# First batch of a fused attention and expert kernel: two exponentials ahead of the router's square, the second batch's maxima behind the choice of the expert, and the rounding of W2 on GpSimd behind the router's index

## The chip, the cores and the metric

One Trainium2 chip, one of its cores, one program. The metric is the device time of a run in microseconds (us). The kernel before takes 421.18 us (median of 3 runs, 421.13 to 421.21).

The engines are named as in the profile: PE is TensorE's matmul stream and PEld its weight loads, DVE is VectorE, ACT is ScalarE, POOL is GpSimd, SP is SyncE, which here only issues transfers. Each engine works its own queue in order; the order is the one in which the program text issues the instructions.

## The reference, cut to what matters

```python
# for each of 8 batches and 8 heads, seq 576, head_dim 64, 32 memory slots
a = exp(phi - phi.max(over seq)); a = a / (a.sum(over seq) + 1e-9)
k_m = a.T @ k ; v_m = a.T @ v                    # 32 x 64 each
s = softmax(q @ k_m.T / 8)                       # 576 x 32
attn_out = s @ v_m                               # 576 x 64
# then tokens x = attn_out laid out as (8*576, 512), 8 experts, F = 1024
logits = (x/|x|) @ (emb/|emb|).T / tau
e = argmax(logits); gate = softmax(logits)[e]
out[mask_e] = gate * (relu(x[mask_e] @ w1[e]) @ w2[e])
```

## The kernel before

The kernel goes through the eight batches one after the other. For batch b it computes with one expert, the one that the batch's tokens name (`choose`, line 160: the tokens are counted on PE, the largest count is read into a register, and W1 and W2 of that expert are loaded). What would be left over for other experts is done in a branch at the end (`rest`), which these inputs don't enter.

The heavy part is two chains of matmuls per batch: `first` (line 617) computes relu(x W1) in 16 steps, and `second` (line 639) multiplies it with W2, token tile by token tile: first the half tile (line 670, W2 unrounded, 32 matmuls), then four whole tiles of 24 matmuls each (line 681). For those, W2 is held as two rounded parts, `wh` (rounded) and `wl` (the rest), in eight chunks; chunk f is needed by the matmuls of step f:

```python
def split_w(self, copy=None):                 # L595
    j = self.halves
    x, h, l = self.w2s[:, j], self.wh[:, j], self.wl[:, j]
    (copy or self.nc.scalar.copy)(h, x)                                        # L598
    self.nc.gpsimd.tensor_tensor(out=l, in0=x, in1=h.bitcast(F32), op=ALU.subtract)  # L599
```

`steps` (line 690) writes the order by hand: two lists, `first` (16 places) and `second` (40 places), hold what is issued behind each step of the two matmul chains, so that softmax, the router and the next batch's attention run beside the matmuls. In batches 1 to 7 all eight `split_w` round on GpSimd (first[0] to first[7]). In batch 0 they round on ScalarE, in first[9], [11], [13], [15] and second[0] to [3], and GpSimd only subtracts.

The start (`moe_linformer`, line 902 on) has no matmul chain to hide behind. Its order: the weights phi of batch 0 are loaded, `largest` (line 411) takes the maxima on VectorE, `softmax` (line 417) the exponentials on ScalarE, for two groups of heads; behind each group one step of `router` (line 313): the square of the expert embeddings on ScalarE (line 319), then the normalisation of them on VectorE (lines 38 to 44 and 324 to 326). `turn` (line 444) transposes the exponentials on PE and copies them back on ScalarE (`eT`); `slots` (line 454) forms k_m and v_m from them and from the keys and values (`kx`, `kl`) in `acc0t` and `acc0m`; then come `block`, `flip`, the scores, the softmax of the first 128 tokens, `attend(0)`, and `choose((0,))`, which releases the load of W1. Batch 1's exponentials, transposes and slots follow, then batch 0's remaining tokens. `warm` (line 344) issues matmuls whose result nobody reads.

`late` (line 225) is the tail of the router for the gates: `root` and `gates` (line 200), handed out over first[3] to first[8] in batch 0. Its last part takes the index of each token's expert, `idx` (line 218), on VectorE from `m` (line 217).

Of the kernel before, what the change touches and what calls it, by code (L numbers as in the profile page):

```python
# [13 lines left out]
ALU = mybir.AluOpType  # L14
# [7 lines left out]
N, DM, E, FF = B * S, H * D, 8, 1024  # L22
NG = 2
# [23 lines left out]
class Tokens:  # L47
# [152 lines left out]
    def gates(self):  # L200
        k, nc, b = self.k, self.nc, self.b
        m, n, lg = self.m, self.n, self.lg
        wk = k.wk.tile

        def b3(x):
            return x.unsqueeze(2).broadcast_to((P, NT, E))

        self.l = l = wk([P, NT, E], F32, tag="l", name=f"l{b}")
        nc.vector.tensor_tensor(out=m, in0=m, in1=n, op=ALU.mult)
        nc.vector.tensor_tensor(out=l, in0=lg, in1=b3(n), op=ALU.mult)  # L210
        nc.vector.tensor_tensor(out=l, in0=l, in1=b3(m), op=ALU.subtract)
        yield
        nc.scalar.activation(l, l, AF.Exp)

        eq = wk([P, NT, E], F32, tag="eq", name=f"eq{b}")
        nc.vector.tensor_tensor(out=eq, in0=self.oh, in1=k.rev8.unsqueeze(1).broadcast_to((P, NT, E)), op=ALU.mult)
        nc.vector.tensor_reduce(out=m, in_=eq, axis=AX.X, op=ALU.max)
        nc.vector.tensor_scalar(out=k.idx[:, b], in0=m, scalar1=-1.0, scalar2=float(E), op0=ALU.mult, op1=ALU.add)
        z = wk([P, NT], F32, tag="zz", name=f"zz{b}")
        nc.vector.tensor_reduce(out=z, in_=l, axis=AX.X, op=ALU.add)  # L220
        nc.vector.tensor_scalar(out=z, in0=z, scalar1=1e-9, scalar2=None, op0=ALU.add)
        nc.vector.reciprocal(out=k.gate[:, b], in_=z)
        yield
# [7 lines left out]
class Kernel:  # L231
# [458 lines left out]
    def steps(self, b, t, u):  # L690


        first, second = ([[] for _ in range(n)] for n in (16, 40))

        for j in range(8):
            copy = self.nc.gpsimd.tensor_copy if b else None
            at = first[j if b else 9 + j * 2] if b or j < 4 else second[j - 4]
            at.append(lambda copy=copy: self.split_w(copy))
        if not b:
            late = t.late()  # L700
            first[2].append(lambda: t.attend(3, 4))
            first[3].append(lambda: t.norm(3, 4))
            first[4] += [t.total, lambda: self.load_kv(2)]

            for f in range(3, 9):
                first[f].append(lambda: next(late))
            first[12] += [lambda: self.keep(0), lambda: self.load_q(2)]
        if u:
            c, o = b + 1, 0 if b else 3
            if not b:  # L710
                first[9].append(lambda: self.scores(c))
            for k in range(2):
                first[(3 + k if b else 9 + 2 * k)].append(lambda k=k: self.results(c, k))

            places = (first[6], first[8], first[10], first[12]), (first[12], first[14], second[0], second[3])
            if not b:
                places = (second[3], second[3], second[3], second[7]), (second[7], second[7], second[7], second[10])
            all = slice(0, BL)
            for g in range(NG):
                work = u.weigh((g,), all)  # L720
                places[g][0].append(lambda g=g: u.fill((g,), all, [self.sT[:, i] for i in range(NG)]))
                for at in places[g][1:]:
                    at.append(lambda work=work: next(work, None))
            for at, g in zip((second[0], second[3]) if b else (second[7], second[10]), range(NG)):
                at.append(lambda g=g: (u.divide((g,), all), u.lay(g), u.turn((g,), all)))
            o = 0 if b else 7
            second[17 + o].append(lambda: u.attend(0, 1, pt=self.mm))
            second[19 + o].append(lambda: u.attend(2, 3))
            second[21 + o].append(lambda: u.attend(4))
            second[22 + o] += [lambda: self.load_w2(u.choose()), self.parts, lambda: self.keep(c)]  # L730
            second[23 + o] += [u.owner, u.flags]
            for n, i in enumerate(((0, 1), (2, 3), (4,)) if b else ((2, 3), (4,), (0, 1))):
                second[24 + n + o].append(lambda i=i: u.norm(*i))
            after = u.late()
            for n in (27, 28, 29, 30, 31, 32):
                second[n + o].append(lambda: next(after))
            second[32 + o].append(lambda: list(after))
            m = b + 2
            if m < B:
                for g in range(NG):  # L740
                    second[11 + 3 * g + o].append(lambda g=g: self.softmax(m, (g,)))
                second[18 + o].append(lambda: self.shares(m))
                second[(28 if b else 25) + o].append(lambda: [self.turn(m, i, min(i + 4, 9)) for i in (0, 4, 8)])
                at = second[(31 if b else 28) + o]
                at += [lambda: self.slots(m), lambda: self.blocks(m, 0), lambda: self.blocks(m, 1, True)]
                for g in range(NG):
                    second[(35 + 2 * g if b else 31 + g) + o].append(lambda g=g: self.flip(m, g))
        return first, second
# [153 lines left out]
def moe_linformer(ctx, tc, phiT, qT, kv, kvt, emb, tau, w1, w2, out):  # L902
    k = Kernel(ctx, tc, phiT, qT, kv, kvt, emb, tau, w1, w2, out)
# [13 lines left out]
    router = k.router()  # L917
    for g in range(NG):
        k.largest(0, g)
        k.softmax(0, (g,))  # L920
        next(router)
    for i in (0, 4, 8):
        k.turn(0, i, min(i + 4, 9))
        if i < 8:
            k.warm(2)
    k.shares(0)
    k.load_phi(1)
    t = Tokens(k, 0, k.pt)
    keys, values = slice(0, 1), slice(1, 2)
    for ks in ((0, 1), (4,), (2,), (3,)):  # L930
        k.slots(0, accs, ks=ks, first=0 in ks, last=3 in ks)
        if ks[0] < 3:
            k.warm(1)
    k.block(0, 0)
    k.load_kv(1)
    k.flip(0, 0, keys)
# [2 lines left out]
    first, others = slice(0, 4), slice(4, BL)  # L939
# [12 lines left out]
    k.warm(5, 2)  # L952
    t.divide(range(NG), first)
    t.turn(range(NG), first)
    k.largest(1, 0)
    k.softmax(1, (0,))
    t.attend(0, pt=lambda shape, name: k.mm(shape, name, 2), turned=False)
    e = t.choose((0,))
    k.largest(1, 1)
    k.softmax(1, (1,))  # L960
    k.load_q(1, (0,))
    t.turned(0)
    for i in (0, 4, 8):
        k.turn(1, i, min(i + 4, 9))
        k.turns += not i
        if not i:
            k.warm(8, hot=t.spare)
    t.fill(range(NG), others, ts)
    weights = [t.weigh((g,), others) for g in range(NG)]
    for g in range(NG):  # L970
# [22 lines left out]
    for b in range(B):  # L993
        u = Tokens(k, b + 1, k.pt) if b < B - 1 else None
        left = k.batch(b, t, u)
        t = u
# [30 lines left out]
```

## Time and profile before

| | |
|---|---|
| median of 3 runs | 421.18 us (421.13 to 421.21) |
| the profiled execution's own time | 421.38 us |
| its span, first to last instruction | 419.0 us |
| PE busy | 405.8 us (97%) |
| DVE / ACT / POOL busy | 262.4 / 173.2 / 168.6 us |
| mean granted TensorE clock | 0.992 |
| first matmul of `first`, batch 0 | 34.48 us |
| first whole tile of `second`, batch 0 | 54.12 us |

The times of the table's last rows count from the start of the span. The profiled execution took 2.4 us more than its span, and 0.20 us more than the median of the runs.

### The profile page before, as it was taken

How to read it: one execution, taken by the hardware profiler on the slowest of the kernel's cores; microseconds unless marked ns; L12 is line 12 of the kernel's file. 1: busy time of each engine (PE TensorE's matmuls, PEld its weight loads, DVE VectorE, ACT ScalarE, POOL GpSimd, SP SyncE). 2: the span in 40 equal slices, each digit the busy share in tenths (PEclk: the TensorE clock that was granted, in tenths of full speed). 3: DMA queues.
4: the chain of work that ended last, by engine and by line, in shares of the span. 5: the costliest groups of instructions: out<-in, count | busy, mean ns of one | idle time of the engine just before them, and what ended most of it. 6: DMA issues, size and time to landing. Idle time of an engine off the chain costs nothing. (4 is left out here: it accounts for less than half of the span.)

```text
span 419.0 us, 9431 instructions
## 1 busy us (share of the span) xinstructions
PE 405.8 (97%) x3489; PEld 329.5 (79%) x3489; DVE 262.4 (63%) x839; ACT 173.2 (41%) x476; POOL 168.6 (40%) x196
## 2 busy tenths in 40 slices
PE   6989999999999999999999999999999999999993
PEld 2458878788877978879787988879788888879783
DVE  4597796679664795648772695648955495745000
ACT  4466742375225722356313642357223661145110
POOL 0032380387132942259130960339331681359000
PEclk9899999999999999999999999999999999999998
DMA  8979926896769824995469926798349404690101
GB/s 272 345 281 344 362 85 156 283 371 268 154 214 398 334 50 118 344 372 218 75 206 378 364 89 148 241 386 318 60 127 366 155 0 96 201 398 10 37 36 47
DMA packets 69858, 91.19 MB, mean 218 GB/s; under 512 B 41800, under 2 KB 47688, under 8 KB 69808
## 3 DMA queue, kind: packets, MB, share of 16 engines
q1 hardware_dynamic: 66928, 82.00, 59.3%
q0 software_dynamic: 2688, 8.26, 5.3%
q8 instruction: 29, 0.48, 0.5%
q10 hardware_dynamic: 192, 0.28, 0.3%
q14 instruction: 21, 0.17, 0.1%
HBM read 71.19 MB, written 19.33 MB: 216 GB/s over the span
## 5 line engine op out<-in xcount | busy, mean ns | idle before, releaser
L628 PE MATMUL ph<-aT,gh 128*128 128x288 f32 x512 | 103.2, 297 | 0.5 <-DVE gl L612 0.5
L681 PE MATMUL py<-wh,hh 128*128 128x512 f32 x248 | 102.3, 413 | 0.0
L681 PE MATMUL py<-wl,hh 128*128 128x512 f32 x248 | 97.0, 391 | 0.3 <-POOL wl L599 0.3
L681 PE MATMUL py<-wh,hl 128*128 128x512 f32 x248 | 97.1, 392 | 0.0
L599 POOL TENSOR_TENSOR wl<-w2s,wh 128x512 fp32r<-128x512 f32 x64 | 83.4, 1306 | 16.8 <-ACT wh L598 12.3
L628 PEld LDWEIGHTS ph<-aT,gh 128*128 128x128 f32 x512 | 81.7, 188 | 3.0 <-DVE gl L612 1.4
L628 PE MATMUL ph<-aT,gl 128*128 128x288 f32 x256 | 75.4, 294 | 0.0
L634 DVE SCALAR_TENSOR_TENSOR hl<-ph,hh 128x288 fp32r<-128x288 f32 x128 | 56.0, 449 | 22.6 <-ACT hh L631 16.6
L631 ACT ACTIVATE hh<-ph 128x288 fp32r<-128x288 f32 x128 | 52.4, 417 | 32.9 <-PE ph L628 32.3
L686 ACT ACTIVATE ys<-py,gate 128x512 f32<-128x512 f32 (+1 forms) x39 | 25.0, 641 | 96.0 <-issue 48.3
L789 POOL DMA_DIRECT2D out_dram<-ys x28 | 15.5, 553 | 118.2 <-ACT ys L686 110.5
L681 PEld LDWEIGHTS py<-wh,hh 128*128 128x128 f32 x248 | 46.6, 188 | 12.0 <-issue 3.9
L681 PEld LDWEIGHTS py<-wh,hl 128*128 128x128 f32 x248 | 46.5, 188 | 10.2
L681 PEld LDWEIGHTS py<-wl,hh 128*128 128x128 f32 x248 | 46.7, 188 | 8.5 <-POOL wl L599 0.7
L628 PEld LDWEIGHTS ph<-aT,gl 128*128 128x128 f32 x256 | 48.0, 188 | 0.0
L589 POOL TENSOR_TENSOR aT<-aw,aT 128x576 fp32r<-128x576 f32 (+3 forms) x20 | 24.5, 1240 | 43.9 <-PE py L681 33.8
L612 DVE TENSOR_TENSOR gl<-pg,gh 128x512 fp32r<-128x512 f32 x32 | 20.0, 683 | 34.9 <-ACT gh L611 34.9
L598 POOL CAST wh<-w2s 128x512 fp32r<-128x512 f32 x56 | 37.5, 669 | 0.6 <-DMA w2s<-w 0.6
L670 PE MATMUL py<-w2s,h 128*64 128x256 f32 x256 | 29.4, 382 | 0.0
L427 ACT ACTIVATE ex<-ex,nm 128x576 f32<-128x576 f32 x16 | 12.3, 770 | 30.9 <-DVE nm L412 29.9
L670 PEld LDWEIGHTS py<-w2s,h 128*64 128x64 f32 x256 | 17.7, 137 | 9.4 <-DVE hl L634 1.1
L119 DVE TENSOR_REDUCE lg<-po 128x8 f32<-128x16 f32 x40 | 6.8, 173 | 28.1 <-PE po L114 28.0
(168 smaller groups left out, 522.6 us busy)
## 6 DMA issues: line engine op xcount, KB each, us to landing
kx<-kv SPq DMA_DIRECT2D x32, 512.0 KB, 7.0
w2s<-w SPq DMA_DIRECT2D x32, 512.0 KB, 10.2
w1s<-w SPq DMA_DIRECT2D x28, 512.0 KB, 6.5
out_dram<-ys POOLq DMA_DIRECT2D x28, 256.0 KB, 6.0
qt<-qT SPq DMA_DIRECT2D x12, 576.0 KB, 8.4
ad<-aw SPq DMA_DIRECT2D x8, 576.0 KB, 13.0
td<-x SPq DMA_DIRECT2D x56, 72.0 KB, 2.2
ea<-td SPq DMA_DIRECT2D x7, 512.0 KB, 4.1
```

What stands on the lines that cost most here:

```text
L427: nc.scalar.activation(x, x, AF.Exp, bias=nm[:, g : g + 1], accum_out=sm[:, g : g + 1])
L589: self.nc.gpsimd.tensor_tensor(out=al, in0=a, in1=ah.bitcast(F32), op=ALU.subtract)
L598: (copy or self.nc.scalar.copy)(h, x)
L599: self.nc.gpsimd.tensor_tensor(out=l, in0=x, in1=h.bitcast(F32), op=ALU.subtract)
L612: nc.vector.tensor_tensor(out=self.gl[:, g, f], in0=ps[g], in1=self.gh[:, g, f].bitcast(F32), op=ALU.subtract)
L628: nc.tensor.matmul(p, lhsT=w[:, g, fs], rhs=x[:, g, to], start=g == 0 and k == 0, stop=g == 1 and k == 2)
L631: nc.scalar.activation(self.hh[:, f, to], p, AF.Relu)
L634: nc.vector.scalar_tensor_tensor(out=self.hl[:, f, to], in0=p, scalar=0.0, in1=self.hh[:, f, to].bitcast(F32), op0=ALU.max, op1=ALU.subtract)
L670: nc.tensor.matmul(p[64 * j : 64 * j + 64], lhsT=self.h4[:, f], rhs=self.w2s[:, f, d * j : d * j + d], start=f == 0, stop=f == 7,)
L681: nc.tensor.matmul(p, lhsT=h[:, f, to], rhs=w[:, f], start=f == 0 and k == 0, stop=f == 7 and k == 2)
L686: nc.scalar.activation(y[:, :d], p, AF.Copy, scale=gate[:, i : i + 1])
L789: eng.dma_start(self.out[r : r + P], y)
```

## The change

In the start: both exponentials of batch 0 are issued ahead of the router's square, which moves behind the first transposes; the normalisation moves behind `shares(0)`; some `warm` counts change. For batch 1, both maxima and both exponentials move behind `choose((0,))` and `turned(0)`, and the eight warm matmuls are divided into four and three. In batch 0 the rounding of W2 moves from ScalarE to GpSimd, in first[9] to first[15] and second[0], and `idx` of batch 0 moves from VectorE to GpSimd, which in GpSimd's queue puts it ahead of all eight `split_w`.

```diff
-        nc.vector.tensor_scalar(out=k.idx[:, b], in0=m, scalar1=-1.0, ...)
+        (nc.vector if b else nc.gpsimd).tensor_scalar(out=k.idx[:, b], in0=m, scalar1=-1.0, ...)
...
         for j in range(8):
-            copy = self.nc.gpsimd.tensor_copy if b else None
-            at = first[j if b else 9 + j * 2] if b or j < 4 else second[j - 4]
-            at.append(lambda copy=copy: self.split_w(copy))
+            at = first[j] if b else first[9 + j] if j < 7 else second[0]
+            at.append(lambda: self.split_w(self.nc.gpsimd.tensor_copy))
...
     for g in range(NG):
         k.largest(0, g)
         k.softmax(0, (g,))
-        next(router)
     for i in (0, 4, 8):
         k.turn(0, i, min(i + 4, 9))
+        if not i:
+            next(router)
         if i < 8:
-            k.warm(2)
+            k.warm(2 if i else 4)
     k.shares(0)
+    next(router)
...
         if ks[0] < 3:
-            k.warm(1)
+            k.warm(2 if ks[0] == 2 else 1)
...
     t.turn(range(NG), first)
-    k.largest(1, 0)
-    k.softmax(1, (0,))
     t.attend(0, pt=lambda shape, name: k.mm(shape, name, 2), turned=False)
     e = t.choose((0,))
-    k.largest(1, 1)
-    k.softmax(1, (1,))
+    t.turned(0)
+    for g in range(NG):
+        k.largest(1, g)
+        k.softmax(1, (g,))
     k.load_q(1, (0,))
-    t.turned(0)
+    k.warm(4, hot=t.spare)
     for i in (0, 4, 8):
         k.turn(1, i, min(i + 4, 9))
         k.turns += not i
         if not i:
-            k.warm(8, hot=t.spare)
+            k.warm(3, hot=t.spare)
```

## Rows read from the trace of the kernel before

**Rows 1.** Busy time by stretch of the span (us from its start): length, busy us of PE, PEld, DVE, ACT and POOL with their instruction counts, then granted clock (1.00 is full), DMA share, GB/s. The middle of the kernel.

```profile
55.00:60.00 5.00, 4.71 (x21) 3.61 (x20) 4.84 (x7) 1.37 (x2) 5.00 (x4) 1.00 0.00 0
62.00:110.00 48.00, 48.00 (x427) 39.85 (x426) 36.46 (x111) 20.92 (x59) 20.90 (x24) 1.00 0.81 252
302.00:350.00 48.00, 48.00 (x426) 39.84 (x425) 31.91 (x103) 20.60 (x57) 21.49 (x24) 1.00 0.47 152
```

**Rows 2.** Instructions in order of time, start of the kernel: start us, us, engine, line, operation, out<-in, count, and in brackets the engine's idle time before it and what ended it.

```profile
6.00 0.75 DVE L412 TENSOR_REDUCE nm<-ex 128x1 f32<-128x576 f32 x1 [1.06 <-DMA ex<-phiT]
7.73 0.63 ACT L319 ACTIVATE w2s<-sT 8x512 f32<-8x512 f32 x1 [1.90 <-DMA sT<-emb]
8.36 0.76 ACT L427 ACTIVATE ex<-ex,nm 128x576 f32<-128x576 f32 x1
8.48 0.14 DVE L38 TENSOR_SCALAR eng<-es 8x1 int32<-8x1 int32 x1 [1.74 <-ACT w2s L319]
9.26 1.12 PE L449 MATMUL te<-ident,ex 128*128 128x128 f32 x4 [2.23 <-ACT ex L427]
10.90 0.47 DVE L326 TENSOR_SCALAR w2s<-sT,en 8x512 f32<-8x512 f32 x1
14.54 0.43 PE L469 MATMUL acc0t<-kx,eT 128*32 128x128 f32 x8
```

**Rows 3.** The same columns as rows 1, half-microsecond stretches of the start.

```profile
10.00:10.50 0.50, 0.50 (x3) 0.27 (x2) 0.40 (x4) 0.08 (x1) 0.00 (x0) 0.50 1.04 420
12.50:13.00 0.50, 0.50 (x17) 0.30 (x9) 0.00 (x0) 0.00 (x0) 0.00 (x0) 0.93 1.04 373
21.50:22.00 0.50, 0.00 (x0) 0.00 (x0) 0.42 (x3) 0.50 (x1) 0.00 (x0) 1.00 1.04 426
```

**Rows 4.** The issue of the fourth transfer of batch 0's keys and values on SP's queue, from the order of time, and the same transfer in the list of transfers, whose last number is us from issue to landing; then the same two for the two halves of batch 0's W1.

```profile
5.28 0.61 SPq L375 DMA_DIRECT2D kx<-kv  x1
kx<-kv SPq DMA_DIRECT2D x1, 512.0 KB, 6.7
23.71 1.37 SPq L397 DMA_DIRECT2D w1s<-w  x2
w1s<-w SPq DMA_DIRECT2D x2, 1024.0 KB, 5.4
```

**Rows 5.** In order of time, from the choice of the expert to batch 0's first heavy matmul.

```profile
20.74 0.71 DVE L412 TENSOR_REDUCE nm<-ex 128x1 f32<-128x576 f32 x1
22.53 0.14 DVE L166 TENSOR_SCALAR seli<-ki 1x1 int32<-1x1 int32 x1
22.60 0.73 DVE L412 TENSOR_REDUCE nm<-ex 128x1 f32<-128x576 f32 x1
23.41 0.78 ACT L427 ACTIVATE ex<-ex,nm 128x576 f32<-128x576 f32 x1 [1.05 <-issue]
25.54 1.08 PE L469 MATMUL acc0t<-kx,eT 128*32 128x128 f32 x32
30.00 1.09 PE L609 MATMUL pg<-w1s,vT 64*32 64x512 f32 x16
34.48 0.53 PE L628 MATMUL ph<-aT,gh 128*128 128x288 f32 x2
```

**Rows 6.** In order of time, the end of the router in batch 0, and GpSimd around it.

```profile
34.56 1.58 POOL L589 TENSOR_TENSOR aT<-aw,aT 128x288 fp32r<-128x288 f32 x2 [2.28 <-ACT aT L588]
39.78 0.46 DVE L634 SCALAR_TENSOR_TENSOR hl<-ph,hh 128x288 fp32r<-128x288 f32 x1 [0.80 <-ACT hh L631]
45.88 0.20 DVE L217 TENSOR_REDUCE m<-eq 128x5 f32<-128x40 f32 x1
46.64 1.28 POOL L599 TENSOR_TENSOR wl<-w2s,wh 128x512 fp32r<-128x512 f32 x1 [10.50 <-ACT wh L598]
50.97 8.68 POOL L599 TENSOR_TENSOR wl<-w2s,wh 128x512 fp32r<-128x512 f32 x6 [0.66 <-ACT wh L598]
```

**Rows 7.** In order of time on GpSimd, batch 1's rounding and subtracting, the first chunk, the fifth chunk's rounding, and a later rounding beside the VectorE instruction of its time; and, from the groups of lines, a small `tensor_scalar` on GpSimd (count, busy us, mean ns).

```profile
85.62 0.61 POOL L598 CAST wh<-w2s 128x512 fp32r<-128x512 f32 x1 [0.61 <-DMA w2s<-w]
86.32 1.28 POOL L599 TENSOR_TENSOR wl<-w2s,wh 128x512 fp32r<-128x512 f32 x1
93.34 0.61 POOL L598 CAST wh<-w2s 128x512 fp32r<-128x512 f32 x1
96.70 1.16 DVE L72 TENSOR_TENSOR x<-x,mx 128x576 f32<-128x576 f32 x1
97.18 1.16 POOL L598 CAST wh<-w2s 128x512 fp32r<-128x512 f32 x1
L438 POOL TENSOR_SCALAR rs<-sm 128x1 f32<-128x1 f32 x1 | 0.2, 221 | 0.1
```

**Rows 8.** In order of time, VectorE, GpSimd and PE while the first whole tile of `second` runs in batch 0.

```profile
53.74 1.72 DVE L72 TENSOR_TENSOR x<-x,mx 128x576 f32<-128x576 f32 x1
54.12 0.50 PE L681 MATMUL py<-wh,hh 128*128 128x512 f32 x1
57.83 1.81 POOL L599 TENSOR_TENSOR wl<-w2s,wh 128x512 fp32r<-128x512 f32 x1
59.70 0.50 PE L681 MATMUL py<-wl,hh 128*128 128x512 f32 x1 [0.29 <-POOL wl L599]
60.01 0.76 DVE L84 TENSOR_TENSOR x<-x,z 128x576 f32<-128x576 f32 x1
```

More of the change, by code (lines that the diff above doesn't have):

```diff
@@ L217, in gates @@
         nc.vector.tensor_reduce(out=m, in_=eq, axis=AX.X, op=ALU.max)
-        nc.vector.tensor_scalar(out=k.idx[:, b], in0=m, scalar1=-1.0, scalar2=float(E), op0=ALU.mult, op1=ALU.add)
+        (nc.vector if b else nc.gpsimd).tensor_scalar(out=k.idx[:, b], in0=m, scalar1=-1.0, scalar2=float(E), op0=ALU.mult, op1=ALU.add)
         z = wk([P, NT], F32, tag="zz", name=f"zz{b}")
```

## The prediction, made before the changed kernel was run

> **What bounds the kernel now.** I read the stretches first. PE is busy without a gap in the stretches after 62 us, of which an early and a late one stand here [rows 1]. Whatever moves PE's stream at 62 us therefore moves the end by as much, and nothing after it can give it back or absorb it. So only two places count: the start, until the first heavy matmul at 34.48 [rows 5], and the gap that the stretch 55 to 60 shows [rows 1].
>
> The order of time shows the start as one chain. ScalarE waits until 7.73 for the embeddings, squares them, and only then takes the second exponential, at 8.36; its maximum had been ready at 6.75 (6.00 + 0.75). PE has nothing for 2.23 before the transposes at 9.26 [rows 2]. After that pause the granted clock is 0.50 (1.2 GHz), and only from 12.5 on is it near 1.00 (2.4 GHz) again [rows 3]. The slots of batch 0 end with the group at 14.54 [rows 2], the expert is chosen at 22.67 (22.53 + 0.14), and the heavy matmuls follow 12 us later [rows 5].
>
> The gap at 59.70 is PE waiting for the last `wl` chunk: GpSimd subtracts six chunks in a row from 50.97 to 59.65 [rows 6, 8]. So GpSimd is already the limit there, by a little. This is the fact that decides the forecast.
>
> **The start, step by step.** With both exponentials first, the second starts at 6.8 instead of 8.36, and its transposes, 0.90 behind it (9.26 - 8.36) [rows 2], at 7.7 instead of 9.26. PE's pause of 2.23 loses 1.55 to the earlier exponential and most of the rest to the two added warm matmuls, so I expect the clock to stay at 2.4 GHz. The square now falls between two copies of `eT` on ScalarE: 0.63, hidden by the transposes that the second copy waits for. The normalisation takes VectorE 2.9 (8.48 to 10.90 + 0.47) [rows 2]; behind a square that ends near 8.8 it ends near 11.8, and VectorE's next work is the product of the slots, which end after 12. If that cover failed, it would cost what sticks out, some tenths.
>
> How far does that carry? The last slots group needs the fourth `kx` transfer, issued at 5.28 and landed 6.7 later, at 12.0 [rows 4]. PE could be there at about 12, does two warm matmuls, and runs the group at 12.1 to 12.2 instead of 14.54: 2.35 earlier. Below, the transfer bounds it; above, nothing gained there is 0. I take 2.35, since each step has its row, and it carries to the choice of the expert: 20.3 instead of 22.67.
>
> Then the second move takes some back. Before, one maximum of batch 1 (0.71) ran ahead of `lg`, in time in which VectorE would otherwise have waited for PE, and only one stood behind the choice; the second exponential started at 23.41, which is 0.74 behind the choice [rows 5]. Now two maxima stand behind it (0.71 + 0.73), and the second exponential starts 0.78 behind the first: 20.3 + 0.74 + 0.78 = 21.85, which is 1.55 earlier than 23.41, not 2.35. Behind the exponential come the transposes, the slots of batch 1 (25.54) and the projection (30.00), all in one chain. VectorE's own chain, from the second maximum (22.60) on, is 0.71 later relative to the choice by the maximum that now stands in it, so it too comes 1.6 earlier. W1's first half landed at 29.1 (23.71 + 5.4) [rows 4], 0.9 before its use at 30.00; issued behind the choice, it moves by 2.35 if the transfers before it are done, and needs to move by only 0.6 to be there at 28.5. So the heavy matmuls start at **33.0 instead of 34.48: 1.5 gained**. Bounds: 0.5 (a copy or transfer late on the way) and 2.35 (the second move costs nothing).
>
> **The rounding, step by step.** GpSimd is idle from 36.1 (34.56 + 1.58) until 46.64 [rows 6]. In the new order its next instruction is `idx`, and all eight chunks stand behind that. `idx` needs `m`, which VectorE has at 46.08 (45.88 + 0.20). VectorE's way there starts behind `hl` at 39.78, which itself waited for ScalarE and, through it, for PE [rows 6], so `m` moves with PE's stream: 44.58. Hand-over 0.07 (GpSimd to PE takes 0.06: 57.83 + 1.81 to 59.70 [rows 8]), `idx` 0.22 (by a like instruction [rows 7]): the first rounding starts at 44.87.
>
> A chunk costs GpSimd a rounding and a subtraction: in batch 1 the first and the fifth rounding start (93.34 - 85.62)/4 = 1.93 per chunk apart [rows 7]. The eighth subtraction ends 7 x 1.93 + 0.70 + 1.28 = 15.49 after the first rounding starts: 60.36.
>
> To this come collisions with VectorE. The instruction of line 72 has two SBUF operands; it took 1.72 beside GpSimd's subtractions, where the like line 84 took 0.76 with GpSimd free of them, and the subtraction that ran beside the second group's line 72 took 1.81 instead of 1.28, so 0.53 lost; in batch 1 a rounding lost 0.55 (1.16 - 0.61) in the same way [rows 7, 8]. In the new order both line 72s and the first line 84 (60.01, moved 1.5 earlier, to 58.5) lie within GpSimd's stretch: three collisions, 1.6. Two would be 1.1, four (the second group's line 84 too) 2.1.
>
> The Trainium skill, "SBUF — State Buffer", section "SBUF: two separate sides", says that VectorE instructions with two SBUF inputs and GpSimd's take turns at one port pair under a lock held for the whole instruction. By that rule each collision could cost GpSimd the whole 0.76 of the VectorE instruction, 2.3 for three; the rows show 0.53 to 0.55, and the rows decide.
>
> So the last chunk is ready at 60.36 + 1.6 = 61.98 and PE goes on at 62.04, where it did at 59.70 [rows 8]. Before that, PE is at the whole tile at 52.6 (54.12 - 1.5) and waits for the sixth, seventh and eighth chunks in turn. ScalarE is relieved of eight roundings, which buys nothing, since PE waits for no ScalarE work in this stretch.
>
> **The sum.** 62.04 - 59.70 = **2.3 us later**, the gain of 1.5 already counted. On the profiled execution that is 421.38 + 2.3 = 423.7; on the median, 0.20 lower, 423.5.
>
> **The rivals.**
>
> *The router doesn't hold the rounding back: faster.* If `m` came early, or GpSimd could round as W2 arrives, PE would find every chunk ready. Then 1.5 of the start and the 0.29 which PE waited for the last chunk before are gained: 421.2 - 1.8 = 419.4. The point from which it decides: to have the last chunk by 59.65, with three collisions, the first rounding must start by 59.65 - 15.49 - 1.6 = 42.6, which is 2.3 before my 44.87. For it: GpSimd idles for 10 us before its first subtraction [rows 6]. Against it: GpSimd works its queue in order, `idx` stands ahead of the rounding there, and nothing in the change brings `m` forward relative to PE's stream.
>
> *The second move costs nothing and two collisions happen:* gain of 2.35 instead of 1.5, 0.5 less lost: 2.3 - 0.85 - 0.5 = 0.95 later, 422.1, on the edge between same and slower.
>
> *The clock falls in PE's wait.* By the pace above PE waits 1.2 to 1.9 before each of the last three chunks: GpSimd takes 1.93 for a chunk, and with a collision 2.5, where PE uses one up in three matmuls, some 0.7 ((59.70 - 54.12)/8). After 2.23 idle microseconds the granted clock was at 0.50 from about 9.3 to 12.6 [rows 2, 3]. If it falls here for as long, 3.3 us at half speed cost up to 1.65 more: 425.1. Part of it would hide in the waits. Against it: between 21.5 and 22.0 PE did nothing, and the clock stayed at 1.00 [rows 3].
>
> *The start's gain is mostly lost* (a late transfer or a copy on ScalarE that PE waits for): 0.5 instead of 1.5, 424.5.
>
> **How the numbers follow.** The forecast 0.55, the clock 0.13, the lost start 0.10, the cheap second move 0.10, the unheld rounding 0.12. About 0.2% (0.84 us) is what a measurement can tell from no change. Faster is the unheld rounding: 0.12. Same takes half of the cheap second move, and the part of the forecast with no collision losses and a little more gain: 0.12. Slower is the rest, 0.76. The forecast's own range is 422.5 to 424.3 (one to four collisions, the start 0.3 either way). The range for 8 in 10 leaves out the unheld rounding and reaches to the others: 421.6 to 425.2.
>
> **What the new profile would show.** The second exponential at 6.8, transposes at 7.7, clock 1.00 from 9 to 13, the last slots group near 12.2; the choice near 20.3, batch 1's second exponential near 21.9, the first heavy matmul near 33.0. GpSimd idle until about 44.6, then `idx`, then sixteen instructions without a pause until 61 to 62; PE waiting for `wl` three times between 56 and 62. I am wrong if the rounding starts before 43, if PE's stream begins before 32, or if PE doesn't wait for `wl`.

## The result, and the profile after

The changed kernel takes 423.75 us (median of 8 runs, 422.03 to 425.39), the kernel before beside it 420.38 us (8 runs, 418.55 to 421.21): ratio 1.0084, interval 1.0055 to 1.0114. It is slower by 0.8%. Run again beside the experiments it gave 424.37 against 420.92, ratio 1.0095 (1.0065 to 1.0124). Its profiled execution took 424.92, with a span of 423.1 (before: 421.38 and 419.0).

The start after the change, in order of time (columns as in [rows 2]; the last three rows answer to the choice, to batch 1's second exponential and to the first heavy matmul in [rows 5]):

```profile
6.51 0.78 ACT L427 ACTIVATE ex<-ex,nm 128x576 f32<-128x576 f32 x1 [0.67 <-DVE nm L412]
7.43 0.66 PE L449 MATMUL te<-ident,ex 128*128 128x128 f32 x4
9.71 0.43 PE L469 MATMUL acc0t<-kx,eT 128*32 128x128 f32 x8 [0.73 <-DMA kx<-kv]
12.32 0.43 PE L469 MATMUL acc0t<-kx,eT 128*32 128x128 f32 x8
20.31 0.14 DVE L166 TENSOR_SCALAR seli<-ki 1x1 int32<-1x1 int32 x1
21.92 0.76 ACT L427 ACTIVATE ex<-ex,nm 128x576 f32<-128x576 f32 x1
32.89 0.53 PE L628 MATMUL ph<-aT,gh 128*128 128x288 f32 x2
```

The second exponential runs at 6.51 instead of 8.36, the last slots group at 12.32 instead of 14.54, the choice ends at 20.45 instead of 22.67, and the heavy matmuls start at 32.89 instead of 34.48: 1.59 gained.

GpSimd and VectorE around the rounding of W2, in order of time, and then PE; these answer to [rows 6] and [rows 8]:

```profile
44.58 0.20 POOL L218 TENSOR_SCALAR idx<-m 128x5 f32<-128x5 f32 x1 [10.03 <-DVE m L217]
44.85 0.61 POOL L598 CAST wh<-w2s 128x512 fp32r<-128x512 f32 x1
51.52 1.67 DVE L72 TENSOR_TENSOR x<-x,mx 128x576 f32<-128x576 f32 x1
52.53 1.14 POOL L598 CAST wh<-w2s 128x512 fp32r<-128x512 f32 x1
54.71 0.95 DVE L72 TENSOR_TENSOR x<-x,mx 128x576 f32<-128x576 f32 x1
55.00 1.14 POOL L598 CAST wh<-w2s 128x512 fp32r<-128x512 f32 x1
57.85 0.80 DVE L84 TENSOR_TENSOR x<-x,z 128x576 f32<-128x576 f32 x1
58.12 1.66 POOL L599 TENSOR_TENSOR wl<-w2s,wh 128x512 fp32r<-128x512 f32 x1
60.41 1.27 POOL L599 TENSOR_TENSOR wl<-w2s,wh 128x512 fp32r<-128x512 f32 x1
57.54 0.50 PE L681 MATMUL py<-wl,hh 128*128 128x512 f32 x1 [0.85 <-POOL wl L599]
59.83 0.79 PE L681 MATMUL py<-wl,hh 128*128 128x512 f32 x1 [1.25 <-POOL wl L599]
60.42 0.63 PE L681 MATMUL py<-wh,hl 128*128 128x512 f32 x1
61.74 0.79 PE L681 MATMUL py<-wl,hh 128*128 128x512 f32 x1 [0.26 <-POOL wl L599]
```

GpSimd waits 10.03 for `m`, rounds from 44.85 without a pause, and PE waits for the sixth, seventh and eighth chunk. The last one is read at 61.74, where it was 59.70 before: 2.04 later. The matmuls from 59.83 on take 0.79 and 0.63 instead of 0.50 and 0.40 (before, 59.70 and the next matmul at 60.04), and the stretches say why (columns as in [rows 1]):

```profile
8.00:13.00 5.00, 4.24 (x87) 2.06 (x85) 2.83 (x17) 1.09 (x4) 0.00 (x0) 1.00 1.04 379
55.00:60.00 5.00, 2.90 (x11) 1.53 (x10) 4.81 (x8) 0.69 (x1) 4.84 (x6) 0.93 0.07 12
60.00:65.00 5.00, 4.74 (x11) 3.25 (x12) 4.39 (x8) 1.71 (x4) 3.41 (x5) 0.50 0.68 113
66.00:110.00 44.00, 44.00 (x408) 36.47 (x408) 29.37 (x96) 18.12 (x52) 20.93 (x23) 1.00 0.70 246
```

The clock no longer falls in the start (1.00 from 8 to 13, where [rows 3] had 0.50), but it falls behind PE's wait: 0.50 from 60 to 65. Two entries of the forecast's list are seen at once: the late chunk, which was the forecast, and the fall of the clock, which was a rival. From the reading of the last chunk to the end of the span, the same work took 419.0 - 59.70 = 359.3 before and 423.1 - 61.74 = 361.4 after, so the fall cost some 2.1. Together with the 2.04 these are the 4.1 by which the profiled spans differ.

### The profile page after: what moved, and what is told of

Read it like the earlier page. It is cut to its first block, busy times and chain, and to the rows that moved or that the text cites. A ratio compares the mean times of both kernels' runs of the same rounds, so it can differ in the third digit from the quotient of the medians.

```text
span 423.1 us, 9432 instructions
## 1 busy us (share of the span) xinstructions
PE 407.9 (96%) x3491; PEld 330.2 (78%) x3491; DVE 263.4 (62%) x838; ACT 169.4 (40%) x468; POOL 173.7 (41%) x205
## 5 line engine op out<-in xcount | busy, mean ns | idle before, releaser
L681 PE MATMUL py<-wh,hh 128*128 128x512 f32 x248 | 103.5, 417 | 0.0
L681 PE MATMUL py<-wl,hh 128*128 128x512 f32 x248 | 98.5, 397 | 2.4 <-POOL wl L599 2.4
L681 PE MATMUL py<-wh,hl 128*128 128x512 f32 x248 | 98.1, 395 | 0.0
L598 POOL CAST wh<-w2s 128x512 fp32r<-128x512 f32 x64 | 43.5, 679 | 0.9 <-PE pg L609 0.8
L114 PEld LDWEIGHTS po<-vv,aw 128*128 128x128 f32 x160 | 21.8, 189 | 2.5 <-ACT vv L575 0.9
```

Of the source, the lines that this page charges most:

```text
L114: nc.tensor.matmul(po[:, 144 * g : 144 * g + P + E], lhsT=k.aw[:, g, to], rhs=k.vv[:, g], start=True, stop=True)
L681: nc.tensor.matmul(p, lhsT=h[:, f, to], rhs=w[:, f], start=f == 0 and k == 0, stop=f == 7 and k == 2)
```

## The experiments

In each, two lengths are read from the profile: the start (to the first heavy matmul, line 628) and the rest (from there to the end of the span). The kernel before has 34.48 and 384.5, the changed kernel 32.89 and 390.2.

**The new start alone.** The changed kernel with the rounding and `idx` put back.

```diff
-        (nc.vector if b else nc.gpsimd).tensor_scalar(out=k.idx[:, b], ...)
+        nc.vector.tensor_scalar(out=k.idx[:, b], ...)
...
-            at = first[j] if b else first[9 + j] if j < 7 else second[0]
-            at.append(lambda: self.split_w(self.nc.gpsimd.tensor_copy))
+            copy = self.nc.gpsimd.tensor_copy if b else None
+            at = first[j if b else 9 + j * 2] if b or j < 4 else second[j - 4]
+            at.append(lambda copy=copy: self.split_w(copy))
```

> The changed kernel with the rounding of W2 and idx put back as before (ScalarE rounds batch 0, idx on VectorE): only the new start is left. Theory (start gains, held rounding costs): first heavy matmul at 32.9 as in the changed kernel, PE at the last wl chunk near 58.1 (59.70 - 1.6), end 1.6 earlier than the profiled run of before: span near 417.4, time near 419.6. Rival (the new start gains only because the clock stays up, and the moved maxima cost 0.7 of it): the same 419.6, but no faster than those runs of before that took 418.6 to 419.9.

Measured: 418.64 (12 runs, 417.92 to 419.85) against 420.85 (29 runs, 418.63 to 423.21), ratio 0.9952 (0.9934 to 0.9970): faster. From its profile, in order of time:

```profile
17.00 0.58 PE L529 MATMUL tr<-qt,kT 64*32 64x448 f32 x4 [0.61 <-DVE z L82]
21.12 0.14 DVE L166 TENSOR_SCALAR seli<-ki 1x1 int32<-1x1 int32 x1
33.71 0.54 PE L628 MATMUL ph<-aT,gh 128*128 128x288 f32 x2
58.91 0.50 PE L681 MATMUL py<-wl,hh 128*128 128x512 f32 x1 [0.27 <-POOL wl L599]
```

The rest is 418.1 - 33.71 = 384.4, as before the change. So the whole loss sits in the moved rounding and `idx`. This execution's start was 0.8 later than the changed kernel's with the same instructions: the second part of the scores of batch 0 (`tr`) came with a pause ahead of 17.00, and with it everything up to the choice was late. A start varies by this much between executions.

**The rounding alone.** The kernel before with the two edits of the rounding.

```diff
-        nc.vector.tensor_scalar(out=k.idx[:, b], ...)
+        (nc.vector if b else nc.gpsimd).tensor_scalar(out=k.idx[:, b], ...)
...
+            at = first[j] if b else first[9 + j] if j < 7 else second[0]
+            at.append(lambda: self.split_w(self.nc.gpsimd.tensor_copy))
```

> The kernel before with the rounding of W2 on GpSimd behind idx on GpSimd, start unchanged. Theory: first heavy matmul at 34.5 as before, idx near 46.1, the last wl chunk read by PE near 63.3 instead of 59.70, so 3.6 later, and up to 2 more where the clock falls in PE's wait: 424 to 426. Rival (the cost comes from the interplay with the new start): 421 to 422.

Measured: 426.52 (6 runs, 425.33 to 427.96) against 420.85, ratio 1.0147 (1.0115 to 1.0179): slower.

```profile
34.41 0.53 PE L628 MATMUL ph<-aT,gh 128*128 128x288 f32 x2
46.10 0.20 POOL L218 TENSOR_SCALAR idx<-m 128x5 f32<-128x5 f32 x1 [10.03 <-DVE m L217]
63.28 0.59 PE L681 MATMUL py<-wl,hh 128*128 128x512 f32 x1 [0.85 <-POOL wl L599]
```

And one stretch, columns as in [rows 1]:

```profile
65.00:70.00 5.00, 5.00 (x20) 4.08 (x19) 1.14 (x2) 1.65 (x5) 0.57 (x1) 0.80 0.58 125
```

The last chunk is read at 63.28, as the theory had it (63.3), 3.6 later than before the change, with the old start. The clock fell behind the waits here too (0.80 from 65 to 70). The rival that needed the two parts together is out: against the kernel before, the start alone gives -2.2 and the rounding alone +5.7, which add up to 3.5, and the whole change gave 3.4 and 3.5.

**No idle PE in the wait.** The changed kernel with matmuls that nobody reads in PE's three waits.

```diff
+        if not b:
+            for n in (12, 13, 14):
+                second[n].append(self.fill_wait)
...
+    def fill_wait(self):
+        if self.spare_hot is None:
+            self.spare_hot = self.pt([P, 512], "hotw")
+            self.turns += 3
+        self.warm(6, hot=self.spare_hot)
```

> The changed kernel with three times six matmuls whose result nobody reads, ahead of the sixth, seventh and eighth step of the first whole tile, that is in PE's three waits for wl. Theory (the clock falls because PE idles in these waits, and this costs 2): the last chunk is still read near 61.7, the granted clock stays at 1.00 from 60 to 65, span near 421.0, and all runs lie close to 422 to 422.8. Rival (half the clock costs nothing, since PE would wait anyway): span stays near 423.

Measured: 422.48 (12 runs, 421.60 to 424.11) against 420.85, ratio 1.0049 (1.0029 to 1.0069): slower. Stretches of its profile, columns as in [rows 1]:

```profile
55.00:60.00 5.00, 5.00 (x23) 3.08 (x22) 4.83 (x7) 1.10 (x2) 4.76 (x6) 1.00 0.00 0
60.00:65.00 5.00, 4.97 (x22) 2.98 (x21) 4.70 (x10) 0.69 (x1) 4.30 (x5) 1.00 0.48 78
```

The clock stays at 1.00 though GpSimd still works nearly without a pause. The rest is 422.0 - 34.36 = 387.6 instead of 390.2 (in this execution too the start was late, 34.36). Part of these 2.6 lies behind the last instruction, as the first heavy matmul of this run and the last computing instruction of the kernel before, of the changed kernel and of this run show (in this run's file lines 628 and 659 are 629 and 660):

```profile
34.36 0.54 PE L629 MATMUL ph<-aT,gh 128*128 128x288 f32 x2
412.50 0.48 DVE L659 TENSOR_SCALAR ys<-py,gate 128x256 f32<-128x256 f32 x1 [24.66 <-PEq L811]
416.57 0.48 DVE L659 TENSOR_SCALAR ys<-py,gate 128x256 f32<-128x256 f32 x1 [24.66 <-PEq L810]
416.08 0.48 DVE L660 TENSOR_SCALAR ys<-py,gate 128x256 f32<-128x256 f32 x1 [24.63 <-PEq L821]
```

Behind its end the span goes on for 6.0 in the kernel before and in the changed kernel, and for 5.4 here. From the first heavy matmul to its end it is 378.5 before, 384.2 in the changed kernel and 382.2 here. So of the 5.7 by which the rest grew, some 2.0 were the clock's and 3.7 the wait's own. The time from the first heavy matmul to the reading of the last chunk says the same of the wait: 28.85 in the changed kernel against 25.22 before, 3.6 more. The median is 1.9 below that of the changed kernel run again in another series (424.37), and 1.3 below its first one (423.75); the intervals of the ratios still overlap a little, so that the split rests on the profiles.

**PE's pause in the old start filled, nothing moved.**

```diff
-            k.warm(2)
+            k.warm(2 if i else 10)
```

> The kernel before with ten instead of two matmuls without a reader behind the first transposes, which fill PE's pause from 7.0 to 9.2; nothing else is moved. Theory (the pause lets the clock fall, and that is most of what the start loses): granted clock 1.00 up to 15, slots of batch 0 done near 13, first heavy matmul near 32.6, time near 419. Rival (the clock doesn't matter there, the order of the exponential does): first heavy matmul stays near 34.5, time 421.

Measured: 418.83 (12 runs, 418.35 to 419.62) against 420.85, ratio 0.9949 (0.9928 to 0.9969): faster. A stretch of its profile, then two rows in order of time:

```profile
8.00:13.00 5.00, 4.68 (x88) 2.69 (x90) 3.25 (x20) 2.18 (x7) 0.24 (x1) 1.00 1.04 370
20.69 0.14 DVE L166 TENSOR_SCALAR seli<-ki 1x1 int32<-1x1 int32 x1
32.65 0.53 PE L628 MATMUL ph<-aT,gh 128*128 128x288 f32 x2
```

Eight added matmuls without a reader bring the heavy matmuls to 32.65, which is 1.83 earlier than before and as early as with the whole new start. Some 0.3 of it may be luck of this execution, in which the second exponential ran at 8.05 instead of 8.36 although the change touches nothing that it waits for. What the new start gained is therefore, for the most part, what the clock gave back; moving the exponential was one way to keep PE busy. The runs of the new start alone agree: their spans, 416.1 to 418.1, are those of the kernel before in its runs with a mean clock of 0.995 or more, 416.4 to 417.6.

This probably explains the spread of the kernel before as well. Its runs fall into groups by the mean granted clock that each lists. Of the 17 runs of one series, five with 0.996 or 0.997 have spans of 416.4 to 417.2, eight with 0.992 or 0.993 have 418.1 to 418.8, and four with 0.990 have 419.9 to 421.0; the 29 runs of the other series fall the same way (416.4 to 417.6, 418.0 to 419.4, 419.9 to 420.7). With the pause filled, all 12 runs lie at 0.996 or more and 416.5 to 417.8. Only one execution of the kernel before has a profile, and its mean clock of 0.992 puts it with the middle group; that the fast group is the one whose clock stays up in the start is inferred from the mean clocks. The mean alone doesn't say where the clock fell, since it falls behind the last matmul as well, where nothing waits for PE. In the run with the filled pause that is what keeps the mean at 0.996:

```profile
414.00:416.00 2.00, 0.00 (x0) 0.00 (x0) 0.00 (x0) 0.00 (x0) 0.00 (x0) 0.50 0.05 12
```

A part of the gain lies where no profile shows it. Each run lists its time and its span. In the kernel before and in the rounding alone, which both have the old start, the time is 2.1 to 2.8 longer than the span (medians 2.5 and 2.6). With the filled pause, and in all runs with the new start or its first part, it is 1.75 to 1.92 (1.8). So some 0.6 of the 2.0 by which the filled pause lowers the median lie outside the span. Why is open.

**The hold taken away.** The changed kernel with `idx` back on VectorE.

```diff
-        (nc.vector if b else nc.gpsimd).tensor_scalar(out=k.idx[:, b], ...)
+        nc.vector.tensor_scalar(out=k.idx[:, b], ...)
```

> The changed kernel with idx back on VectorE, so that nothing in GpSimd's queue holds the eight roundings of batch 0 until the router is done; the roundings stay on GpSimd. Theory (the hold is what costs; the pace of GpSimd alone would fit): the first rounding starts when W2 lands, near 38 to 41 instead of 44.85, the last chunk is done before 58, PE doesn't wait for wl, the clock stays at 1.00, and from the first heavy matmul to the end the kernel takes 384.0 to 384.5 as the kernel before does: 418 to 419. Rival (GpSimd is too slow, or its collisions with VectorE's router make the router late): PE still waits 1 or more for wl or for the gate, 420 or more.

Measured: 424.47 (6 runs, 423.39 to 425.30) against 420.92, ratio 1.0101 (1.0072 to 1.0130): as slow as with the hold. My theory failed here. In order of time:

```profile
35.13 0.61 POOL L598 CAST wh<-w2s 128x512 fp32r<-128x512 f32 x1 [1.11 <-DMA w2s<-w]
42.04 0.86 DVE L43 SCALAR_TENSOR_TENSOR nrr<-nrr,ss 128x5 f32<-128x5 f32 x1
47.66 1.07 DVE L216 TENSOR_TENSOR eq<-oh,rev 128x40 f32<-128x40 bf16 x1
48.77 0.20 DVE L217 TENSOR_REDUCE m<-eq 128x5 f32<-128x40 f32 x1
51.21 0.54 PE L628 MATMUL ph<-aT,gh 128*128 128x288 f32 x2 [2.36 <-DVE hl L634]
```

And the table of waits from 34 to 66 us (who waited for whom, us in total, times, longest):

```profile
PE ph L628 <- DVE hl L634: 4.4, 4, 2.4
```

The rounding does start when W2 lands (35.13), and no matmul waits for `wl`. But it now runs beside the router's many small VectorE instructions. Line 43 takes 0.86 instead of 0.17, line 216 takes 1.07 instead of 0.19. `m` is ready at 48.97 where the changed kernel had it at 44.49, although the heavy matmuls began 0.5 earlier. `hl`, which VectorE makes between these small instructions, comes late with them, and PE waits 4.4 for it in the middle of `first`. The rest is 421.6 - 32.36 = 389.2, which is 4.7 more than before the change: the hold's 3.7 are exchanged for more than that.

**The maxima put back as well.** As the run just told, with `largest` and `softmax` of batch 1 around the choice as before, and eight warm matmuls in one place.

```diff
     t.turn(range(NG), first)
+    k.largest(1, 0)
+    k.softmax(1, (0,))
     t.attend(0, ..., turned=False)
     e = t.choose((0,))
-    t.turned(0)
-    for g in range(NG):
-        k.largest(1, g)
-        k.softmax(1, (g,))
+    k.largest(1, 1)
+    k.softmax(1, (1,))
     k.load_q(1, (0,))
-    k.warm(4, hot=t.spare)
+    t.turned(0)
...
-            k.warm(3, hot=t.spare)
+            k.warm(8, hot=t.spare)
```

> As the run with idx back on VectorE, and besides batch 1's maxima and exponentials put back to their places around the choice of the expert. Theory (the moved maxima cost 0.7 to 0.8 of the start's gain): from the choice to the first heavy matmul 11.8 to 12.0 as in the kernel before, instead of 12.4 to 12.6, and the kernel is 0.7 to 0.8 faster than its companion: 417.5 to 418. Rival (the chain behind the choice is set by transfers): no difference.

Measured: 424.77 (6 runs, 424.39 to 425.81), ratio 1.0102 (1.0074 to 1.0130). No faster than its companion, so the forecast of the time was wrong; the lengths were right. The choice ends at 19.90 in both (19.76 and 19.77, and 0.14), and the heavy matmuls start at 31.94 instead of 32.36. The gain is lost later: in this profile PE's longest wait for `hl` is followed by a lower clock,

```profile
50.00:55.00 5.00, 4.02 (x17) 4.02 (x18) 3.08 (x10) 1.75 (x7) 0.34 (x1) 0.52 0.21 85
```

and the rest is 424.0 - 31.94 = 392.1, against 389.2 in its companion, where the same wait of 2.36 left the clock at 1.00:

```profile
45.00:50.00 5.00, 2.40 (x15) 1.70 (x13) 4.79 (x13) 2.58 (x12) 4.76 (x6) 1.00 1.05 398
50.00:55.00 5.00, 3.79 (x28) 3.23 (x30) 4.06 (x12) 2.51 (x10) 0.58 (x1) 1.00 0.27 112
```

**Only the exponentials ahead of the square.** The first part of the change alone, without the moved maxima and without the rounding; its diff against the kernel before is the first half of the start's diff (lines 918 to 935 of its file).

> Only the first part of the change: both exponentials of batch 0 ahead of the router's square and the warm counts with it; batch 1's maxima, the rounding and idx as before. Theory: clock 1.00 up to 15, choice near 20.3, first heavy matmul near 32.2, the last chunk's short wait of 0.3 as before, time 417.8 to 418.6. Rival (the order of the exponentials gains nothing beyond the clock): as the kernel before with the filled pause, 418.8 or more.

Measured: 418.23 (12 runs, 417.83 to 419.42) against 420.92, ratio 0.9938 (0.9916 to 0.9961). This beats both kernels.

```profile
19.98 0.14 DVE L166 TENSOR_SCALAR seli<-ki 1x1 int32<-1x1 int32 x1
31.94 0.53 PE L628 MATMUL ph<-aT,gh 128*128 128x288 f32 x2
57.15 0.50 PE L681 MATMUL py<-wl,hh 128*128 128x512 f32 x1 [0.28 <-POOL wl L599]
```

From the end of the choice to the first heavy matmul it takes 31.94 - 20.12 = 11.82, as before the change (11.81); the changed kernel takes 32.89 - 20.45 = 12.44. So moving batch 1's maxima and exponentials, with the matmuls around them, costs 0.62 there. In time the run lies 0.41 under the new start alone and 0.60 under the filled pause, but those were timed in another series, and the intervals overlap. In the profiles the choice ends 0.71 earlier than with the filled pause (20.12 against 20.83), which is what the order of the exponentials may give beyond the clock.

**The changed kernel again.**

> The changed kernel again, unaltered, to have it beside these. Theory (the clock falls in PE's wait in some executions, and transfers of the start vary): 422 to 425.5; the first heavy matmul between 32.9 and 34.4; the last chunk about 28.85 behind the first heavy matmul in every profile (61.74 - 32.89).

Measured: 424.37 (6 runs, 423.85 to 425.45) against 420.92. In order of time:

```profile
33.04 0.54 PE L628 MATMUL ph<-aT,gh 128*128 128x288 f32 x2
61.87 0.63 PE L681 MATMUL py<-wl,hh 128*128 128x512 f32 x1 [0.85 <-POOL wl L599]
```

The last chunk is read 28.83 behind the first heavy matmul, as expected. From there to the end 422.9 - 61.87 = 361.0, again 1.7 more than the 359.3 with the clock up:

```profile
60.00:65.00 5.00, 4.15 (x11) 2.92 (x12) 4.53 (x8) 1.58 (x4) 3.56 (x5) 0.71 0.69 113
```

## Why the prediction was right, and where it was not

The forecast was 423.5, in the range 421.6 to 425.2; measured 423.75.

**The start.** Forecast against profile: second exponential 6.8 and 6.51 (its maximum was ready 0.28 earlier in this execution), transposes 7.7 and 7.43, last slots group 12.1 to 12.2 and 12.32, choice 20.3 and 20.45, batch 1's second exponential 21.85 and 21.92, heavy matmuls 33.0 and 32.89. The bound by the fourth `kx` transfer did not bind in this profile: the last slots group follows its two warm matmuls without a wait. PE waited earlier, for 0.73 ahead of 9.71, for another `kx` transfer. The taking back by the moved maxima, 0.7 to 0.8 in the sum, was 0.62. What the forecast did not see is what its 2.35 consisted of. It put it down to the order of the exponentials and took the clock along as a by-product; the filled pause shows that the clock alone gives 1.5 to 1.8.

**The rounding.** First rounding 44.87 and 44.85; pace 1.93 as read from batch 1; three collisions of 1.6 in all, measured 0.53 + 0.53 + 0.37 = 1.43 (1.14 against 0.61 twice, 1.66 against 1.29); last chunk read at 62.04 and 61.74. (Two sums of the forecast are 0.02 to 0.03 too high, 21.85 and 61.98; this moves nothing.) The rule of the Trainium skill, "SBUF — State Buffer", section "SBUF: two separate sides", that the later of the two engines is blocked, agrees with these rows. Its upper price of 0.76 for each collision does not show: GpSimd lost 0.37 to 0.53. VectorE pays more than GpSimd in the first of these meetings, 1.67 instead of 0.76 for line 72, but it paid that before the change too (1.72 in [rows 8]).

**The clock in the wait.** This was a rival with a chance of 0.13, and it came true: 0.50 and 0.71 from 60 to 65 in the two profiles of the changed kernel, 2.1 and 1.7 lost. It did not come true every time: two of the eight runs list a mean clock of 0.999, so that it can hardly have fallen anywhere, and have spans of 420.2 and 420.8. Still, it should have been the likeliest case, for the forecast itself named three waits with little work between them.

**Why the total still fits.** Here the forecast had luck. Its span was 419.0 + 2.3 = 421.3, and the eight runs list spans of 420.2 to 423.5, in the middle 421.9, so 0.6 more. But it also carried over the 2.4 by which the time of the profiled run exceeded its span, and in the changed kernel this is 1.8 in every run, so 0.6 less. The two cancel. Against the kernel before they don't: the loss was 3.37 (423.75 - 420.38), where the forecast had 2.3. It started from three runs at 421.2 and a profile in which the clock falls in the start, and other runs of the kernel before are up to 2.6 faster (418.55). That the clock varies between executions on both sides, from run to run, was not in the sum.

**The rival that failed.** "The router doesn't hold the rounding back: faster", 419.4, assumed that GpSimd's collisions were confined to lines 72 and 84. Taken on its own terms, with the rounding free to start, the kernel takes 424.47. The step that failed is the count of collisions: an earlier rounding meets the router, and there the price is not GpSimd's 0.5 but VectorE's, which has `hl` behind it in its queue and PE behind that (4.4 of waits). So the hold has a use: it keeps the rounding away from the router. But it ends too late for the eight chunks.

**What stays open.** Five profiles have the changed kernel's start, and their first heavy matmuls lie between 32.36 and 34.36. In the two late ones (33.71 and 34.36) the matmuls of `tr` come in two bunches with a pause of 0.61, as if the last part of q had come late. The landing of that transfer stands in no trace, so this is a guess. The time outside the span, 2.5 with the old start and 1.8 with the new one, has no cause yet. The third group of the kernel before (spans of 419.9 to 421.0) has no profile.

## What to carry to other kernels

Where PE is packed to the end, price a move to another engine by that engine's pace from the moment its inputs exist to the last chunk that PE reads, and not by whether the engine is idle. Before a gain in an early, loosely filled stretch is put down to a new order, fill PE's pause with matmuls that nobody reads, since that alone may give it. And moving GpSimd's work to another time, to spare a wait, gains nothing if VectorE has work at that time which it slows and for which PE waits.

## What the runs showed of the hardware that I had not expected

The granted clock can fall after several short waits too, and not only after one long one: in the changed kernel PE was busy for 2.90 of the 5 us from 55 to 60, with single waits of 1.25 or less by the rows, and the clock was at 0.50 from 60 to 65. With warm matmuls in those waits it stayed at 1.00. Nor does the same wait always have the same end: behind a wait of 2.36 it stayed at 1.00 in one kernel (`idx` back on VectorE) and was at 0.52 in the other (the maxima put back as well). And it differs between executions of one program: over 17 runs the kernel before listed mean clocks from 0.990 to 0.997, with spans from 421.0 down to 416.4.

With GpSimd rounding and subtracting without a pause beside them, many of VectorE's instructions on 128x5 and 128x40 elements took 0.5 to 1.2 instead of 0.15 to 0.2 (lines 43, 44, 209, 211, 216 and 221 in the run with `idx` back on VectorE). A small instruction can so be held up for nearly the whole of the large one that it meets: 1.22 at most, beside subtractions of 1.26 to 1.30. Not every one was: the reciprocals of line 42 kept 0.17 to 0.18.
